# Linear attention plus a gated MLP on one core: loads on three queues, twelve tiles transposed by DMA, list order by landing times, the last tile in two pieces

## The chip, the core and the metric

The kernel runs on one core of a Trainium2 chip. The core has five engines with an instruction list each: TensorE (PE in the profile; its weight loads are shown apart as PEld), VectorE (DVE), ScalarE (ACT), GpSimd (POOL) and SyncE (SP), which here only issues DMAs. They meet through semaphores. Sixteen DMA engines move data between the chip's memory (HBM) and the core's on-chip memory, and within the latter. The metric is the device time of one execution, in microseconds (us).

## The reference

```
xn = (x - mean) / sqrt(var + 1e-5)                  # x: 2048 tokens x 512
# A: linear attention, 32 heads of 16
q, k, v = heads(xn @ wqkv)
pq, pk  = q @ w_phi[h], k @ w_phi[h]
phi(p)  = concat(softmax(p), softmax(-p))           # 32 features per head
kv, z   = sum_s phi(pk)^T v, sum_s phi(pk)
A       = (phi(pq) @ kv / (phi(pq) @ z + 1e-6)) @ wo
# B: gated MLP, F = 1792
B       = ((xn @ w_gate) * (xn @ w_up)) @ w_down
out     = x + A + B
```

All inputs and the output are bfloat16.

## The kernel before

Tokens are handled in 16 tiles of 128, one token per partition. A TensorE product needs the normalised tokens transposed (`xnT`: features on partitions). The stages:

- *Normalisation.* `emit_ln_stats` (L403) takes the statistics of a batch of tiles on VectorE (L406, L408), adds the epsilon on VectorE (L412) and raises to the power -1/2 on POOL (L414). The batches (L640) are tiles 0, 1, 2, 3 alone, then 4 to 7, 8 to 11, 12 to 15. `emit_xn` (L427) scales a tile on VectorE (L428) into a ring of four, transposes it on TensorE by four 128x128 products with the identity, and ScalarE copies the result from PSUM into `xnT`.
- *Weights folded.* `wprime` (L438) multiplies the transposed query and key weights (`wT`, loaded by a transposing DMA) with block-diagonal copies of `w_phi` (`wbd`, made on POOL, L384) into `Wp`, so that one product gives pq or pk.
- *Keys.* For each tile: V (`k_pe`), pk (`k_pk`), and `emit_exp` (L451): ScalarE copies p and -p, VectorE takes the maximum over features in a tree (L464), subtracts it (L470), ScalarE takes the exponential. `emit_sums` (L476) adds up in a tree on VectorE (L484); `k_norm` divides (L508, L511). `emit_kv` adds phi(pk)^T [v, 1] over eight tiles at a time.
- *MLP.* `glu` (L520) computes for a group g of four tiles and a block ft of 128 hidden units the gate and up products (eight matmuls of 512 columns); ScalarE copies the gate, VectorE multiplies (L533).
- *Queries.* `q_pk`, `emit_exp`, `q_scale`, a transposing DMA of the features (`q_T`), the products with kv (`q_num`), the division (L602, L603), a transposing DMA of the result (`q_oT`).
- *Output.* `final` (L616) accumulates 14 products with `w_down` and four with `wo`, 18 matmuls of 512 columns; VectorE adds x (L635) and SP stores the tile.

Each operation is recorded once with what it reads and writes (`_Sched`); nearly all matmuls thus carry the line L292, ScalarE's operations L273, DMA issues L162 (transposing) or L163. `_order` (L696) then plans: it goes through time with a price and a latency for each step, and on each engine takes the step that can start first, and among equals the one with the lowest priority number. Without an explicit priority that is the order of recording; `glu` has numbers from 1e6, `final` from 2e6, so that these two fill TensorE when nothing earlier is ready. A DMA is priced with 500 ns to issue, its bytes at 385 per ns behind what is queued, and 1400 ns:

```python
queued = dma_free > start + DMA_ISSUE + 200.0
dma_free = max(dma_free, start + DMA_ISSUE) + st.nbytes / DMA_RATE
st.finish = dma_free + DMA_LAT + (1000.0 if queued else 0.0)
```

The order that comes out is fixed in the program: at run time each engine goes through its list in that order and waits at each step for the semaphores that it needs.

All loads but the small `w_phi` are issued by SP, in this order: x tiles 0 to 1, 2 to 3, V weights, key weights (transposing), gate and up columns 0 to 511, x 4 to 7, query weights (transposing), x 8 to 15, the remaining gate and up columns, `w_down`, `wo`. TensorE starts with 50 products of a zeroed tile (L364), on which nothing depends.

Of the kernel before, what the change touches and what calls it, by code (L numbers as in the profile page):

```python
# [7 lines left out]
ACTF = mybir.ActivationFunctionType  # L8
# [58 lines left out]
class _Step:  # L67
    __slots__ = ("eng", "fn", "idx", "deps", "sig", "lane", "semval", "known", "waits", "is_out", "cost", "lat",
                 "seq", "finish", "prio", "nbytes")

    def __init__(self, eng, fn, idx, lane):
# [15 lines left out]
        self.nbytes = 0  # L87


class _Sched:  # L90
# [65 lines left out]
    def dma(self, eng, out_ap, in_ap, is_out=False, transpose=False, nbytes=131072, prio=None):  # L156
# [10 lines left out]
        st.nbytes = nbytes  # L167
# [26 lines left out]
def _build(nc, es, A_x, A_wqkv, A_w_phi, A_wo, B_w_gate, B_w_up, B_w_down, out):  # L194
# [73 lines left out]
    def act_op(out_ap, in_ap, func=ACTF.Copy, scale=1.0, bias=None, prio=None):  # L268
# [10 lines left out]
        return sc.step(ACT, fn, reads=r, writes=[out_ap], cost=50.0 + 0.833 * in_ap.free_size(), lat=180.0, prio=prio)  # L279
# [4 lines left out]
    def pool(fn, reads, writes, n, rate=2.0, prio=None):  # L284
        return sc.step(POOL, fn, reads=reads, writes=writes, cost=130.0 + rate * n, lat=120.0, prio=prio)
# [45 lines left out]
    def load_x(t0, n):  # L331
        sc.dma(SP, sbv("x", t0 * 512, n * 512).rearrange("p (t d) -> p t d", t=n),
               x_flat[t0 * 128:(t0 + n) * 128, :].rearrange("(t p) d -> p t d", p=128), nbytes=n * 131072)

    def load_w(dst, src, nbytes):
        sc.dma(SP, dst, src, nbytes=nbytes)

    def load_wT(w):

        sc.dma(SP, wT_v[:, w, :, :], A_wqkv[:, w * 512:(w + 1) * 512], transpose=True, nbytes=524288)  # L340

    def load_gu(f0, n):
        for v, src in ((wg_v, B_w_gate), (wu_v, B_w_up)):
            load_w(v[:, :, f0 * 128:(f0 + n) * 128],
                   src[:, f0 * 128:(f0 + n) * 128].rearrange("(q p) f -> p q f", p=128), n * 131072)

    sc.dma(ACT, wphi_v, bass.AP(tensor=A_w_phi.tensor, offset=A_w_phi.offset, ap=[[16, 128], [2048, NQ], [1, 16]]),
           nbytes=16384)
    load_x(0, 2)
    load_x(2, 2)  # L350
    load_w(wv_v, A_wqkv[:, 1024:1536].rearrange("(q p) j -> p q j", p=128), 524288)
    load_wT(1)
    load_gu(0, 4)
    load_x(4, 4)
    load_wT(0)
    load_x(8, 8)
    load_gu(4, 10)
    load_w(wd_v, B_w_down.rearrange("(f p) j -> p f j", p=128), NF * 131072)
    load_w(wo_v, A_wo.rearrange("(q p) j -> p q j", p=128), 524288)


    warm = sbv("tree", 0, 128)
    dve(lambda e: e.memset(warm, 0.0), [], [warm], 128)
    mms([(bank(7, 0, 128), warm, warm, True, True)] * 50, warm=True)  # L364
# [18 lines left out]
    for jt in range(NQ):  # L383
        pool(lambda e, jt=jt: e.tensor_tensor(  # L384
            out=wbd_v[:, jt, :].rearrange("p (g f b) -> p g f b", g=2, b=4),
            in0=wphi_v[:, jt, None, :, None].to_broadcast([128, 2, 16, 4]),
            in1=bind8.rearrange("p (g b) -> p g b", g=2)[:, :, None, :].to_broadcast([128, 2, 16, 4]), op=ALU.mult),
            [bind8, wphi_v[:, jt, :]], [wbd_v[:, jt, :]], 128)
# [3 lines left out]
        [maskh], [eps4], 4)  # L392

# [9 lines left out]
    def emit_ln_stats(t0, n):  # L403
# [3 lines left out]
        for t in range(t0, t0 + n):  # L407
# [4 lines left out]
        dve(lambda e: e.tensor_scalar(out=veps.unsqueeze(2), in0=var4, scalar1=1e-5, scalar2=None, op0=ALU.add),  # L412
            [mv_v[:, ts, :]], [veps], n)
        pool(lambda e: e.tensor_tensor(out=rstd4, in0=veps.unsqueeze(2), in1=mhalf[:, 0:n].unsqueeze(2), op=ALU.pow),  # L414
             [veps, mhalf], [rstd_v[:, ts, 0:1]], n, rate=150.0)
# [176 lines left out]
    def q_T(t):  # L592
        sc.dma(SP, eT(t), eq(t), transpose=True, nbytes=2 * 262144)
# [15 lines left out]
    def q_oT(t):  # L609
        o = sbv("oring", (t % 2) * 512, 512)  # L610
        sc.dma(SP, oT_v[:, :, t * 128:(t + 1) * 128], o, transpose=True, nbytes=2 * 131072)
# [36 lines left out]
    for t0, n in batches:  # L648
        emit_ln_stats(t0, n)
        for t in range(t0, t0 + n):  # L650
            emit_xn(t)
            k_pe(t)
# [183 lines left out]
```

## Time and profile before

| | us |
|---|---|
| three runs, median (lowest, highest) | 229.64 (229.61, 229.78) |
| the profiled execution | 230.12 |
| its span, from the first to the last instruction | 228.0 |
| TensorE busy | 219.0 |
| VectorE busy | 193.7 |
| ScalarE busy | 119.7 |
| POOL busy | 8.2 |

The profile is of one execution. The busy time of TensorE counts matmuls that overlap in its pipeline, so the pace is better read from the starts of weight loads. In a timeline a row merges neighbouring instructions of one kind on one engine: start, length, engine, line, operation, output and inputs, number; in brackets the idle time of the engine before it, and what ended that. The strip of DMA digits gives the busy share of the sixteen DMA engines in 40 slices of 5.7 us, in tenths. In the list of DMA issues the last number of a row is the median time from the issue's start to the landing.

### The profile page before, as it was taken

The page shows a single profiled execution, that of the slowest core. Times are in us where ns is not written, and L with a number is a line of the kernel's source. Part 1 is how long each engine was busy: PE and PEld are TensorE (multiplying, and loading weights), DVE is VectorE, ACT ScalarE, POOL GpSimd, SP SyncE. Part 2 cuts the span into 40 slices and gives each one's busy share as a digit, 9 for nine tenths or more (in the row PEclk, how much of TensorE's full clock was granted, in tenths as well). Part 3 has the DMA queues.
Part 4 walks back from the last instruction along what each step waited for, and adds up shares of the span by engine and source line. Part 5 has one row for each costly group of instructions (what it writes and reads, how often), then busy time and mean ns, then how long its engine had stood idle before and what let it go on. Part 6 is the DMA issues. An engine that isn't in the chain of part 4 may idle for free.

```text
span 228.0 us, 3617 instructions
## 1 busy us (share of the span) xinstructions
PE 219.0 (96%) x1306; PEld 108.9 (48%) x1330; DVE 193.7 (85%) x554; ACT 119.7 (52%) x201; POOL 8.2 (4%) x22
## 2 busy tenths in 40 slices
PE   8899799999999999999999999999999999998994
PEld 8454354444454555444464444444445444444441
DVE  4548999999997999999986999999999999993321
ACT  2587997735449987944528585464653331110000
POOL 5301000000011000000000000000000000000000
PEclk9999999999999999999999999999999999999999
DMA  6999970000000000000000035554144545468301
GB/s 181 249 285 369 379 249 1 0 0 0 0 3 1 0 3 0 0 3 0 0 4 0 0 65 96 85 94 103 36 92 105 118 92 116 92 126 110 88 23 46
DMA packets 39697, 18.33 MB, mean 80 GB/s; under 512 B 30720, under 2 KB 38656, under 8 KB 39680
## 3 DMA queue, kind: packets, MB, share of 16 engines
q1 hardware_dynamic: 39152, 18.09, 32.5%
q8 instruction: 10, 0.16, 0.3%
q10 hardware_dynamic: 528, 0.02, 0.1%
q14 instruction: 7, 0.06, 0.1%
HBM read 8.67 MB, written 2.10 MB: 47 GB/s over the span
## 4 chain that ended last, share of the span: by engine, by line
PE 85%; SPq 6%; DMA 5%; DVE 1%; issue 1%; ACT 1%
PE ps L292 85%; SPq L162 4%; DMA arena<-in_A_x_dram 3%; DMA arena<-arena 2%; SPq L163 1%; ACT arena L273 1%; DVE arena L464 1%; DVE arena L406 0%; DVE arena L635 0%; DVE arena L470 0%
## 5 line engine op out<-in xcount | busy, mean ns | idle before, releaser
L292 PE MATMUL ps<-arena 128*128 128x512 bf16 (+3 forms) x1306 | 219.0, 328 | 6.1 <-ACT arena L273 2.4
L292 PEld LDWEIGHTS ps<-arena 128*128 128x128 bf16 x1330 | 108.9, 100 | 115.7 <-DVE arena L533 2.3
L273 ACT ACTIVATE arena<-ps 128x512 bf16<-128x512 f32 (+1 forms) x168 | 88.0, 590 | 50.6 <-PE ps L292 45.7
L484 DVE TENSOR_TENSOR arena<-arena 128x512 f32<-128x512 bf16 (+3 forms) x128 | 49.3, 395 | 0.2
L273 ACT ACTIVATE arena<-arena 128x1024 bf16<-128x1024 bf16 x32 | 34.0, 1061 | 29.0 <-DVE arena L470 28.1
L533 DVE TENSOR_TENSOR arena<-ps,arena 128x512 bf16<-128x512 f32 x56 | 38.1, 681 | 2.2 <-PE ps L292 1.6
L464 DVE TENSOR_TENSOR arena<-arena 128x128 bf16<-128x128 bf16 (+3 forms) x128 | 31.7, 269 | 2.2 <-ACT arena L273 2.0
L470 DVE TENSOR_TENSOR arena<-arena 128x1024 bf16<-128x1024 bf16 x32 | 21.6, 676 | 0.0
L635 DVE TENSOR_TENSOR arena<-ps,arena 128x512 bf16<-128x512 f32 x16 | 11.0, 688 | 11.8 <-PE ps L292 11.5
L406 DVE BATCH_NORM_STATS2 arena<-arena 128x6 f32<-128x512 bf16 x16 | 10.5, 682 | 6.8 <-DMA arena<-in_A_x_dram 6.8
L603 DVE TENSOR_TENSOR arena<-ps,arena 128x512 bf16<-128x512 f32 x16 | 10.9, 680 | 0.1
L511 DVE TENSOR_TENSOR arena<-arena 128x1024 bf16<-128x1024 bf16 x16 | 10.9, 680 | 0.0
L602 DVE RECIPROCAL arena<-ps 128x32 f32<-128x32 f32 x16 | 5.6, 350 | 4.6 <-PE ps L292 4.3
L508 DVE RECIPROCAL arena<-arena 128x64 bf16<-128x64 f32 x16 | 8.7, 543 | 0.1
L428 DVE TENSOR_SCALAR arena<-arena 128x512 bf16<-128x512 bf16 x16 | 5.9, 409 | 2.2 <-POOL arena L414 2.0
L414 POOL TENSOR_TENSOR arena<-arena 128x1 f32<-128x1 f32 (+1 forms) x7 | 5.2, 750 | 60.7 <-DVE arena L412 60.7
L589 DVE TENSOR_TENSOR arena<-arena 128x512 bf16<-128x512 bf16 x16 | 6.6, 414 | 0.0
L586 DVE RECIPROCAL arena<-arena 128x32 f32<-128x32 f32 x16 | 5.5, 342 | 0.0
L587 DVE TENSOR_TENSOR arena<-arena 128x32 bf16<-128x32 f32 x16 | 2.7, 171 | 0.0
L273 ACT ACT_TABLE_LOAD x1 | 1.3, 1283 | 1.3 <-PEq L821 1.3
L408 DVE BATCH_NORM_AGGREGATE arena<-arena 128x2 f32<-128x6 f32 x16 | 1.9, 162 | 0.0
L551 DVE TENSOR_TENSOR arena<-arena 128x64 bf16<-128x64 f32 x8 | 1.7, 214 | 0.0
(18 smaller groups left out, 8.4 us busy)
## 6 DMA issues: line engine op xcount, KB each, us to landing
out_dram<-arena SPq DMA_DIRECT2D x16, 128.0 KB, 1.7
arena<-in_B_w_down_dram SPq DMA_DIRECT2D x1, 1792.0 KB, 15.4
arena<-in_B_w_gate_dram SPq DMA_DIRECT2D x1, 1280.0 KB, 9.1
arena<-in_B_w_up_dram SPq DMA_DIRECT2D x1, 1280.0 KB, 11.9
arena<-in_A_x_dram SPq DMA_DIRECT2D x1, 1024.0 KB, 6.5
arena<-in_A_x_dram SPq DMA_DIRECT2D x2, 256.0 KB, 3.2
arena<-in_A_wqkv_dram SPq DMA_DIRECT2D x1, 512.0 KB, 5.2
arena<-in_B_w_gate_dram SPq DMA_DIRECT2D x1, 512.0 KB, 4.4
```

Source lines behind the costliest of these rows:

```text
L162: return e.dma_start_transpose(out_ap, in_ap)
L273: return e.activation(out=out_ap, in_=in_ap, func=func, scale=scale, **kw)
L292: ins = e.matmul(o, lhsT=l, rhs=r, start=a, stop=z)
L406: dve(lambda e, t=t: e.bn_stats(stats_v[:, t, 0:6], x_tile(t)), [x_tile(t)], [stats_v[:, t, 0:6]], 512)
L464: dve(lambda e, dst=dst, src=src, k=k: e.tensor_tensor(out=dst, in0=src[:, :, 0:k], in1=src[:, :, k:2 * k], op=ALU.max), [src], [dst], 16 ...
L470: dve(lambda e: e.tensor_tensor(out=p4, in0=p4, in1=src[:, :, None, :].to_broadcast([128, 16, 16, 4]), op=ALU.subtract), [pst, src], [pst] ...
L484: dve(lambda e, dst=dst, src=src, k=k: e.tensor_tensor(out=dst, in0=src[:, :, 0:k], in1=src[:, :, k:2 * k], op=ALU.add), [src[:, :, 0:2 * ...
L508: dve(lambda e: e.reciprocal(out=rs, in_=sm), [sm], [rs], 64, rate=8.0)
L511: dve(lambda e: e.tensor_tensor(out=e4, in0=e4, in1=r4[:, :, None, :].to_broadcast([128, 16, 16, 4]), op=ALU.mult), [ek_v[:, t, :], rs], [ ...
L533: dve(lambda e: e.tensor_tensor(out=dst, in0=bank(bu), in1=gr, op=ALU.mult), [bank(bu), gr], [dst], 512, prio=-1.0)
L603: dve(lambda e: e.tensor_tensor(out=o.rearrange("p (g h d) -> p g h d", g=8, h=4), in0=nd[:, :, 0:64].rearrange("p g (h d) -> p g h d", h= ...
L635: dve(lambda e: e.tensor_tensor(out=og, in0=bank(b), in1=x_tile(t), op=ALU.add), [bank(b), x_tile(t)], [og], 512, prio=-2.0)
```

## The change

- The loads are spread over three queues. SP: x tile 0, tile 1, tiles 2 to 3, key weights, query weights (both transposing). ScalarE: `w_phi`, V weights, x 4 to 7, gate and up columns 0 to 511. POOL: x 8 to 15, the remaining gate and up columns, `w_down`, `wo`; these five are made to wait for the landing of x 4 to 7 and for the last `wbd` product.
- ScalarE gets a first Exp of a zeroed element; the warm-up has 46 products instead of 50.
- The four `wbd` products on POOL move behind the power of tile 3, each behind POOL's step before it.
- The epsilon is added on POOL instead of VectorE.
- Tiles 4 to 15 are transposed by a DMA on SP; tiles 0 to 3 stay on TensorE.
- The planner no longer models the bytes: each load carries a time `at` at which it is taken to have landed, each issue a price, each transposing DMA a latency. Prices of some ScalarE, POOL and reciprocal steps are changed.
- In `final` the three matmul pieces have one priority, and tile 15 is computed and stored in two pieces, columns 0 to 383 and 384 to 511, in two PSUM banks.

The diff, cut to its core:

```diff
-    def dma(self, eng, out_ap, in_ap, is_out=False, transpose=False, nbytes=131072, prio=None):
+    def dma(self, eng, out_ap, in_ap, is_out=False, transpose=False, issue=500.0, land=1700.0, at=0.0, prio=None):
...
+        st.cost = issue
+        st.lat = land
+        st.at = at
...
-        return sc.step(ACT, fn, reads=r, writes=[out_ap], cost=50.0 + 0.833 * in_ap.free_size(), lat=180.0, prio=prio)
+        return sc.step(ACT, fn, reads=r, writes=[out_ap], cost=(50.0 if str(in_ap.tensor.name) == "ps" else 95.0) + 0.833 * in_ap.free_size(),
+                       lat=180.0, prio=prio)
...
-    def pool(fn, reads, writes, n, rate=2.0, prio=None):
-        return sc.step(POOL, fn, reads=reads, writes=writes, cost=130.0 + rate * n, lat=120.0, prio=prio)
+    def pool(fn, reads, writes, n, rate=1.8, fixed=130.0, prio=None):
+        return sc.step(POOL, fn, reads=reads, writes=writes, cost=fixed + rate * n, lat=120.0, prio=prio)
...
+    def load_w(on, dst, src, at):
+        return sc.dma(on, dst, src, at=at, issue=500.0 if on != POOL else 850.0)
+
+    def load_wT(w, at):
+
+        sc.dma(SP, wT_v[:, w, :, :], A_wqkv[:, w * 512:(w + 1) * 512], transpose=True, at=at, issue=4600.0)
...
+    load_x(SP, 0, 1, 2900.0)
+    load_x(SP, 1, 1, 3500.0)
+    load_x(SP, 2, 2, 4500.0)
+    load_wT(1, 9500.0)
+    load_wT(0, 15000.0)
     sc.dma(ACT, wphi_v, bass.AP(tensor=A_w_phi.tensor, offset=A_w_phi.offset, ap=[[16, 128], [2048, NQ], [1, 16]]),
-           nbytes=16384)
-    load_x(0, 2)
-    load_x(2, 2)
-    load_w(wv_v, A_wqkv[:, 1024:1536].rearrange("(q p) j -> p q j", p=128), 524288)
-    load_wT(1)
-    load_gu(0, 4)
-    load_x(4, 4)
-    load_wT(0)
-    load_x(8, 8)
-    load_gu(4, 10)
-    load_w(wd_v, B_w_down.rearrange("(f p) j -> p f j", p=128), NF * 131072)
-    load_w(wo_v, A_wo.rearrange("(q p) j -> p q j", p=128), 524288)
-
-
-    warm = sbv("tree", 0, 128)
-    dve(lambda e: e.memset(warm, 0.0), [], [warm], 128)
-    mms([(bank(7, 0, 128), warm, warm, True, True)] * 50, warm=True)
+           at=4200.0)
+    one = sbv("lnt", 4 * NT, 1)
+    zero = sbv("tree", 0, 128)
+    dve(lambda e: e.memset(zero, 0.0), [], [zero], 128)
+    act_op(one, zero[:, 0:1], func=ACTF.Exp)
+    load_w(ACT, wv_v, A_wqkv[:, 1024:1536].rearrange("(q p) j -> p q j", p=128), 6500.0)
+    x4_loaded = load_x(ACT, 4, 4, 9000.0)
+    load_gu(ACT, 0, 4, 12500.0)
+
+
+    mms([(bank(7, 0, 128), zero, zero, True, True)] * 46, warm=True)
...
+    def make_wbd():
+        for jt in range(NQ):
+            pool(lambda e, jt=jt: e.tensor_tensor(
...
+                [bind8, wphi_v[:, jt, :]], [wbd_v[:, jt, :]], 128).deps.append(sc.by_eng[POOL][-2])
+
+    def load_rest():
+        wbd_made = sc.by_eng[POOL][-1]
+        late = [load_x(POOL, 8, 8, 15500.0)]
+        late += load_gu(POOL, 4, 10, 23000.0)
+        late.append(load_w(POOL, wd_v, B_w_down.rearrange("(f p) j -> p f j", p=128), 30000.0))
+        late.append(load_w(POOL, wo_v, A_wo.rearrange("(q p) j -> p q j", p=128), 32000.0))
+        for st in late:
+            st.deps += [x4_loaded, wbd_made]
...
-        dve(lambda e: e.tensor_scalar(out=veps.unsqueeze(2), in0=var4, scalar1=1e-5, scalar2=None, op0=ALU.add),
-            [mv_v[:, ts, :]], [veps], n)
+        pool(lambda e: e.tensor_scalar(out=veps.unsqueeze(2), in0=var4, scalar1=1e-5, scalar2=None, op0=ALU.add),
+             [mv_v[:, ts, :]], [veps], n)
...
+        if t >= 4:
+            sc.dma(SP, xnT_v[:, :, t * 128:(t + 1) * 128], xn_tile(t), transpose=True, issue=1250.0, land=3200.0)
+            return
         b = next_a()
...
-        dve(lambda e: e.reciprocal(out=rs, in_=sm), [sm], [rs], 64, rate=8.0)
+        dve(lambda e: e.reciprocal(out=rs, in_=sm), [sm], [rs], 64, rate=6.0)
...
-        sc.dma(SP, eT(t), eq(t), transpose=True, nbytes=2 * 262144)
+        sc.dma(SP, eT(t), eq(t), transpose=True, issue=1250.0, land=3300.0)
...
-        sc.dma(SP, oT_v[:, :, t * 128:(t + 1) * 128], o, transpose=True, nbytes=2 * 131072)
+        sc.dma(SP, oT_v[:, :, t * 128:(t + 1) * 128], o, transpose=True, issue=1250.0, land=3200.0)
...
+        c0, c1 = cols
+        ob = bank(b, c0, c1 - c0)
+        items = [(hT(g, ft, lo, 128), wd_v[:, ft, c0:c1]) for ft in range(NF)]
+        items += [(oT_v[:, q, t * 128:(t + 1) * 128], wo_v[:, q, c0:c1]) for q in range(NQ)]
+        items = group(ob, items)
+        for k in (0, 7, 14):
+            mms(items[k:k + 7], prio=base)
...
+        if t0 == 3:
+            make_wbd()
+            load_rest()
...
-    for t in range(NT):
+    for t in range(NT - 1):
         final(t, 7 if t < 4 else (7, 5, 6)[t % 3])
+    final(NT - 1, 7, (0, 384))
+    final(NT - 1, 5, (384, 512))
...
-            free_at[e] = start + DMA_ISSUE
-            queued = dma_free > start + DMA_ISSUE + 200.0
-            dma_free = max(dma_free, start + DMA_ISSUE) + st.nbytes / DMA_RATE
-            st.finish = dma_free + DMA_LAT + (1000.0 if queued else 0.0)
+            free_at[e] = start + st.cost
+            st.finish = max(start + st.lat, st.at)
```

## The prediction

> **What bounds the kernel now.** I read the page first, then the chain of work that ended last, then the timeline of TensorE's weight loads (PEld; every matmul has one, and none is missing), and last the timelines of SP and VectorE in the first 26 us.
>
> From the page: the span, TensorE's share, the idle time before matmuls, the DMA queues and two landings.
>
> ```profile
> span 228.0 us, 3617 instructions
> PE 219.0 (96%) x1306; PEld 108.9 (48%) x1330; DVE 193.7 (85%) x554; ACT 119.7 (52%) x201; POOL 8.2 (4%) x22
> DMA  6999970000000000000000035554144545468301
> ...
> PE 85%; SPq 6%; DMA 5%; DVE 1%; issue 1%; ACT 1%
> ...
> arena<-in_A_x_dram SPq DMA_DIRECT2D x1, 512.0 KB, 6.2
> arena<-arena SPq DMA_TRANSPOSE x32, 3.1
> arena<-in_A_wqkv_dram SPq DMA_TRANSPOSE x2, 7.8
> ```
>
> TensorE works 96% of the span and carries 85% of the chain: only what takes work or idle time off TensorE, or shortens what stands before its first and after its last matmul, can pay. VectorE (85%) is the next bound. The sixteen DMA engines are full from slice 2 to slice 6 (up to 34 us) and nearly idle until 131 us.
>
> TensorE's weight loads at the start and at the end, from the timeline:
>
> ```profile
> 6.73 0.23 PEld L292 LDWEIGHTS ps<-arena 128*128 128x128 bf16 x4 [0.44 <-DVE arena L428]
> 7.26 0.23 PEld L292 LDWEIGHTS ps<-arena 128*128 128x128 bf16 x4 [0.30 <-DVE arena L428]
> ...
> 18.85 3.90 PEld L292 LDWEIGHTS ps<-arena 128*128 128x128 bf16 x28 [0.70 <-DVE arena L428]
> 24.86 1.22 PEld L292 LDWEIGHTS ps<-arena 128*128 128x128 bf16 x10 [2.10 <-DVE arena L533]
> ...
> 208.01 2.31 PEld L292 LDWEIGHTS ps<-arena 128*128 128x128 bf16 x19 [1.30 <-DMA arena<-arena]
> ...
> 218.03 6.57 PEld L292 LDWEIGHTS ps<-arena 128*128 128x128 bf16 x31
> ```
>
> The last row gives the rate: 30 steps in 6.47 us, 0.216 us for a 512-column matmul. The first two give the price of a transpose on TensorE: four in 0.23 us. Between 25 and 225 us TensorE stands still for one wait worth the name (the 1.30 before 208.01); at the start there are two (0.70, 2.10), and in both the releaser is VectorE.
>
> Why VectorE is late there, from the timelines of SP and VectorE:
>
> ```profile
> 2.32 4.54 SPq L162 DMA_TRANSPOSE arena<-in_A_wqkv_dram  x1
> ...
> 8.07 0.51 SPq L163 DMA_DIRECT2D arena<-in_A_x_dram  x1
> 8.62 5.39 SPq L162 DMA_TRANSPOSE arena<-in_A_wqkv_dram  x1
> ...
> 17.82 7.99 SPq L163 DMA_DIRECT2D arena<-in_A_wo_dram  x1
> ```
>
> ```profile
> 14.30 2.47 DVE L406 BATCH_NORM_STATS2 arena<-arena 128x6 f32<-128x512 bf16 x4 [4.78 <-DMA arena<-in_A_x_dram]
> ...
> 18.39 1.38 DVE L428 TENSOR_SCALAR arena<-arena 128x512 bf16<-128x512 bf16 x4 [0.53 <-POOL arena L414]
> 19.69 0.42 DVE L464 TENSOR_TENSOR arena<-arena 128x512 bf16<-128x512 bf16 x1
> ```
>
> One queue issues all loads. The load of tokens 4 to 7 goes out at 8.07 us, behind a weight transpose that holds the queue for 4.54 us, and lands at 14.3. VectorE has idled 4.78 us by then, does the statistics of these tiles, and only at 19.69 starts the softmax work of the first tile. From there it is busy to about 209 us.
>
> **The change part by part.** Gains are against the profiled execution, whose time is 230.12 us for a span of 228.0; the median of the three runs, 229.64, is 0.48 lower, and I take the same gain off it.
>
> *Start.* Four warm-up matmuls fewer are 4 x 0.107 = 0.43 us (the 50 of before take 5.41). TensorE also idles 0.27 between the warm-up and the first transposes. Tile 0, loaded alone, should land between 2.5 us (0.8 plus 1.7, the page's landing of a 128 KB store) and the 3.9 of the two-tile load; I take 3.3. Then statistics 0.69 and 0.16, POOL 0.2 for the added epsilon (small POOL rows are 0.10 to 0.19) and 0.55 for the power, scaling 0.47, hand-overs 0.2: 5.6, before the warm-up ends at 6.0. Gain 0.7, bounds -0.4 and 0.7: the warm-up steps by 0.107 where the transposes after it step by 0.057, and if the faster pace came no earlier than before, at 6.7, real work would run at half pace until then. Of the smaller waits up to 11 us (0.30, 0.33, 0.48) I count 0.4 as gained, since tiles 2 and 3 come while earlier products run.
>
> *Transposes.* Tiles 4 to 15 lose four transposes each: 12 x 0.23 = 2.7 us of TensorE, and ScalarE 12 evictions of 0.6, which are hidden (ScalarE is busy 52%). In their place SP issues 12 DMA transposes. The 32 of before land after 3.1 us, idle DMA engines about them; tiles 8 to 15 find this too (slices 8 to 23 are empty), and the matmuls of loaded tiles cover them. Tiles 4 to 7 fall into the full slices: 3.1 at best, 7.8 at worst by the weight transposes. These move four times the bytes, so I take 4.
>
> *Tokens 4 to 7, three queues.* On ScalarE's queue wv goes out after the table load (1.30 plus 1.28), x 4 to 7 next, then the first gate and up columns; these issues (0.5 each) and the early Exp (0.24) lie in ScalarE's idle 4.59 us before 7.17. By order alone x 4 to 7 take the place of the first gate load, which landed at 6.91 + 4.4 = 11.3; right behind wv (1.82 + 5.2 = 7.0) they would land at 8.5, as 512 KB follow each other by 1.45 (gate 11.3, up 12.8, x 14.3). I take 9.5, as the issue no longer waits for the weight transpose.
> The Trainium skill's page "DMA: Bandwidth & Descriptors", section "Issuing engines are not separate DMA queues", says that several issuing engines save only the time the sequencer takes to issue, as all loads run on the same DMA engines. By it I would take the 11.3, and the sum below would be some 1.8 smaller.
>
> POOL now waits for x 4 to 7 and for its own wbd products (1.47, moved behind the fourth power), then issues five loads; behind these, in its order as the planner's prices put it, stand the epsilon and power of tiles 4 to 7, for which xn 4 to 7, SP's transposes and the products of tile 4 wait. No POOL issue is in this trace. Bounds from SP's rows: 0.5 each, and 7.99 where the queue is full. I take the planner's own 0.85, near the many short rows: 9.5 + 4.25 = 13.8, power 1.2 with epsilon, scaling 0.5, transpose 4: tile 4 lies transposed at 19.5. The statistics (2.8) hide beside the issues. TensorE's other work up to there: 6.0 + tiles 0 to 3 transposed 0.9, their V and score products 6.9, W' for keys 0.9, four gate-up pairs 6.9, W' for queries 0.9, bubbles 1 = 23.5. So there is cover, but the lists run in order, and the planner (landing 3.2) puts tile 4's product near 18: 0.9 of new waits, bounds 0 and 13.
> The Trainium skill's page "SBUF — State Buffer", section "Who interferes with whom", has VectorE in its two-port modes shut GpSimd out, descriptor writing included. If the four scalings (0.41 each) and no more did this, it would be 1.6 later; no run here shows it yet.
>
> With x 4 to 7 done early the waits of 0.70 (for xn 4) and 1.64 (TensorE's own idle time under the 2.10) go: 2.3. Late next is VectorE's softmax chain, which should start near 14.5, after the first score product, some 5 us earlier, less 1.2 for the scalings that now follow.
>
> *Order elsewhere.* The planner's new prices cost nothing themselves, they only move list entries. Seven epsilon additions (1.1) leave VectorE. I take nothing for this, nor for the 1.30 before 208 (a transpose of 4.9 instead of 3.1); bounds -2 and +1.3.
>
> *Last tile.* Eighteen matmuls of 512 become 18 of 384 and 18 of 128: 3.9 both ways, weight loads at 0.057 keeping pace. The last addition falls from 0.69 to about 0.28 (between 0.21 for 65 columns and 0.41 for 256); the first piece's addition and store run beside the second piece. The last store stays at 1.7. Gain 0.4.
>
> Sum: 0.7 + 0.4 + 2.7 + 2.3 - 0.9 + 0.4 = 5.6: 224.5 against 230.12, 224.0 against the median.
>
> **Rivals.**
> *VectorE holds the end.* In the profile 14.2 us of TensorE work follow the last numerator product (210.9 to 225.1), which waits for VectorE's chain. If that chain starts only 3 us earlier (x 4 to 7 at 11.3), TensorE's savings turn into waits for it: 3 + 0.4 gives 226.2. For it: VectorE is busy 176 of the 189 us between 25 and 214. Against: finals can be put ahead of the last numerators, and TensorE has work to spare there.
> *Tiles 4 to 7 late, the other sign.* POOL's issues block as SP's did at 17.82. With three issues of 0.85, one of 7.99 and one more, POOL is free at 20.9, tile 4 transposed at 25 or later, and TensorE, in order, waits from about 18.5: 6.5 us. The 2.3 are not gained then, 3.3 of gains remain: 229.64 + 3.2 = 232.8. It is slower from a wait of 3.3 us on, tile 4 transposed after 22. For it: 5.9 MB queued at once. Against: most issue rows are half a microsecond.
> *A smaller wait of this kind*, 2 us more than I took: 226.0.
> *The loads gain nothing*: the DMA engines are full either way, tokens 4 to 7 still land past 13, and the transposes' 2.7 return as waits on landings: 229.4.
>
> **How the numbers follow.** Forecast 0.58, with a range of its own of 222.3 to 225.5; VectorE 0.16; the smaller wait 0.12; the late tiles 0.11; no gain 0.03. All gains at once, with the 1.30 and no new wait, are 5.6 + 0.9 + 1.3: 221.8, so I start the range a little under that, at 221.3, and end it at 228.3, which leaves out the slower case, the no-gain case and little else. A difference of under 0.2% (0.46 us; the three runs span 0.17) can't be told from none. Faster 0.86, same 0.03, slower 0.11.
>
> **What would show it.** Statistics of tile 4 before 10 us, not 14.30; POOL's five issues done by 14; no transposes on TensorE past tile 3; weight loads of tile 4's V product without an idle row over 1 us; no 2.10 near 24.86; first softmax row of VectorE near 14.5; last addition under 0.3. Wrong, if a wait on a DMA landing over 3 us stands on TensorE between 16 and 30 us, or if TensorE idles before numerator products from 195 us on.

## The result and the profile after

| | before | changed |
|---|---|---|
| median of the runs, us (lowest, highest) | 229.71 (229.61, 229.94) | 243.31 (242.55, 243.77) |
| the profiled execution, us | 230.12 | 242.55 |
| its span, us | 228.0 | 241.1 |

The changed kernel takes 1.059 times as long (95% interval 1.057 to 1.061): 13.6 us slower, where 5.6 us less had been forecast. One execution of a later kernel (246.12 us, under "Both, and the last tile's pieces in order") fell in a slower state of the chip and is left out of that kernel's median. The first reading is the page of the changed kernel.

```profile
span 241.1 us, 3562 instructions
...
PE 220.8 (92%) x1273; PEld 106.4 (44%) x1296; DVE 192.0 (80%) x548; ACT 114.4 (47%) x190; POOL 14.4 (6%) x34
...
PEclk9799756999999999999999999999999999999999
DMA  6999990000000440000000035465336356762101
...
PE 57%; DVE 23%; DMA 12%; issue 3%; ACT 3%; SPq 0%; DVEq 0%
```

VectorE and ScalarE are busy a little less than before. What is new is in the strip of the granted TensorE clock: a dip in slice 2 (6 to 12 us) and one in slices 5 to 7 (24 to 42 us). From the page of the kernel before, the same strip, all nines, and the row of its two-tile loads of x for comparison further down:

```profile
PEclk9999999999999999999999999999999999999999
...
arena<-in_A_x_dram SPq DMA_DIRECT2D x2, 256.0 KB, 3.2
```

And the chain that ended last, 85% TensorE before, now runs through DMA landings (12%) and VectorE (23%). The list of waits (engine and line, what it waited for, total in us, times, longest) names the events:

```profile
PEld ps L296 <- DMA arena<-arena: 13.5, 5, 9.7
...
DVE arena L501 <- ACT arena L276: 12.8, 3, 11.7
...
PEld ps L296 <- DVE arena L442: 3.2, 1, 3.2
```

The 9.7 is a wait for a DMA from on-chip memory to on-chip memory: a transpose of a token tile. VectorE's 11.7 is its echo, since VectorE then has no scores to work on. The 3.2 is at the start, for the scaling of tile 0. First the start, from the timeline:

```profile
7.37 1.29 DVE L420 BATCH_NORM_STATS2 arena<-arena 128x6 f32<-128x512 bf16 x2 [2.59 <-DMA arena<-in_A_x_dram]
8.57 0.72 DVE L442 TENSOR_SCALAR arena<-arena 128x512 bf16<-128x512 bf16 x2
9.02 0.59 PEld L296 LDWEIGHTS ps<-arena 128*128 128x128 bf16 x8 [3.15 <-DVE arena L442]
...
10.94 0.15 PEld L296 LDWEIGHTS ps<-arena 128*128 128x128 bf16 x1 [0.28 <-issue]
...
13.48 1.12 POOL L164 DMA_DIRECT2D arena<-in_A_x_dram  x1 [0.63 <-POOL arena L393]
...
14.11 0.24 PEld L296 LDWEIGHTS ps<-arena 128*128 128x128 bf16 x4 [0.48 <-DMA arena<-in_A_wqkv_dram]
...
17.18 0.76 POOL L164 DMA_DIRECT2D arena<-in_A_wo_dram  x1
...
20.18 11.75 SPq L163 DMA_TRANSPOSE arena<-arena  x4
21.03 0.42 DVE L481 TENSOR_TENSOR arena<-arena 128x512 bf16<-128x512 bf16 x1
```

VectorE's list has the statistics of tiles 2 and 3 ahead of the scaling of tile 0 (L442). The planner had been told that these tiles land at 4.5 us; they land at 7.3. TensorE idles 3.15 us after its warm-up, starts its transposes at 9.02 (6.73 before), and then runs at half pace: from 10.51 to 12.64 us its weight loads start 0.43 us apart instead of 0.216, and the granted clock is 0.50 there. The list of DMA issues shows what else is late:

```profile
arena<-in_A_x_dram SPq DMA_DIRECT2D x1, 256.0 KB, 5.6
...
arena<-in_A_wqkv_dram SPq DMA_TRANSPOSE x2, 9.2
```

Two tiles of x took 5.6 us (3.2 before), the transposed weights 9.2 (7.8 before); the key weights landed at 13.8 us (TensorE's row at 14.11 waits for them), where they had landed at 8.9. They lost that time to ScalarE's loads, packet by packet: between 8.5 and 11.5 us the DMA records of SP's queue hold 786 packets of 256 bytes of the key weights, those of ScalarE's queue 750 of 1024 bytes. From 13 to 14.5 us, with no other queue at work, 1682 packets of 256 bytes go by, over four times the rate. Then tile 4, on the weight loads:

```profile
33.18 0.13 PEld L296 LDWEIGHTS ps<-arena 128*128 128x128 bf16 x2 [9.66 <-DMA arena<-arena]
...
35.98 0.13 PEld L296 LDWEIGHTS ps<-arena 128*128 128x128 bf16 x2 [1.81 <-DMA arena<-arena]
36.38 0.15 PEld L296 LDWEIGHTS ps<-arena 128*128 128x128 bf16 x1 [0.28 <-issue]
```

The four transposes were issued from 20.18 on (the SPq row above) and landed at 33.1, 35.9, 36.4 and 36.8: 13 us for the first, against 2.4 to 4.3 for tiles 8 to 15 later in the same execution. The 0.28 in the last row, repeated for each load up to 40 us, is the half pace: a step of 0.43 instead of 0.216. The granted clock stood at half from 26.5, while TensorE still waited, to 40.2. Windows of the two kernels (length, busy time with instruction counts of PE, PEld, DVE, ACT, POOL, granted clock, DMA share, GB/s), the changed one first:

```profile
25.00:47.00 22.00, 12.85 (x57) 5.68 (x59) 9.12 (x26) 9.14 (x16) 0.00 (x0) 0.69 0.57 148
47.00:79.00 32.00, 31.59 (x145) 13.19 (x147) 32.00 (x83) 17.30 (x27) 1.28 (x2) 1.00 0.02 4
```

```profile
25.00:47.00 22.00, 21.84 (x115) 10.57 (x117) 21.95 (x57) 18.62 (x32) 0.00 (x0) 1.00 0.37 122
47.00:79.00 32.00, 31.84 (x165) 15.17 (x166) 30.32 (x83) 19.91 (x34) 2.02 (x2) 1.00 0.00 1
```

From 25 to 47 us TensorE gets through 59 weight loads instead of 117. From 47 to 79 VectorE is busy without a gap, 32.00 of 32, and TensorE gets through 147 where there were 166: the score work that VectorE could not do during the wait now holds TensorE up. In the starts of weight loads the delay against before is 2.3 us at the first transposes, 3.6 at the scores of tile 3 (17.41 to 21.05), 14.5 at the first hidden units of group 1 (51.69 to 66.18), and 12.9 at the end; the transposes that left TensorE give a little back on the way.

At the end nothing is gained either:

```profile
237.81 0.76 DVE L647 TENSOR_TENSOR arena<-ps,arena 128x384 bf16<-128x384 f32 x2 [3.02 <-PE ps L296]
```

The two pieces of the last tile were interleaved on TensorE, so both additions come at the very end, one behind the other. From TensorE's last result to the end of the span it is 3.1 us, against 2.9 before.

### The profile page after: what moved, and what is told of

Same layout as the page of the kernel before. It is cut to its first block, busy times and chain, and to the rows that moved or that the text cites. A ratio compares the mean times of both kernels' runs of the same rounds, so it can differ in the third digit from the quotient of the medians.

```text
span 241.1 us, 3562 instructions
## 1 busy us (share of the span) xinstructions
PE 220.8 (92%) x1273; PEld 106.4 (44%) x1296; DVE 192.0 (80%) x548; ACT 114.4 (47%) x190; POOL 14.4 (6%) x34
## 4 chain that ended last, share of the span: by engine, by line
PE 57%; DVE 23%; DMA 12%; issue 3%; ACT 3%; SPq 0%; DVEq 0%
PE ps L296 57%; DMA arena<-arena 9%; DVE arena L550 7%; DVE arena L501 5%; DVE arena L481 3%; ACT arena L276 3%; DMA arena<-in_A_x_dram 2%; DVE arena L487 2%; DVE arena L525 1%; DVE arena L528 1%; DVE arena L442 1%; DVE arena L420 1%; DVE arena L620 1%; DVE arena L606 0%; DVE arena L603 0%
## 5 line engine op out<-in xcount | busy, mean ns | idle before, releaser
L296 PE MATMUL ps<-arena 128*128 128x512 bf16 (+4 forms) x1273 | 220.8, 334 | 17.2 <-DMA arena<-arena 10.8
L296 PEld LDWEIGHTS ps<-arena 128*128 128x128 bf16 x1296 | 106.4, 100 | 131.4 <-DMA arena<-arena 13.5
L276 ACT ACTIVATE arena<-ps 128x512 bf16<-128x512 f32 (+1 forms) x156 | 82.4, 584 | 63.2 <-PE ps L296 55.6
L501 DVE TENSOR_TENSOR arena<-arena 128x512 f32<-128x512 bf16 (+3 forms) x128 | 50.3, 397 | 12.9 <-ACT arena L276 12.8
L276 ACT ACTIVATE arena<-arena 128x1024 bf16<-128x1024 bf16 (+1 forms) x33 | 34.1, 1035 | 30.2 <-DVE arena L487 28.5
L550 DVE TENSOR_TENSOR arena<-ps,arena 128x512 bf16<-128x512 f32 x56 | 38.2, 683 | 5.5 <-ACT arena L276 4.9
L647 DVE TENSOR_TENSOR arena<-ps,arena 128x512 bf16<-128x512 f32 (+2 forms) x17 | 11.0, 654 | 15.8 <-PE ps L296 15.8
L528 DVE TENSOR_TENSOR arena<-arena 128x1024 bf16<-128x1024 bf16 x16 | 10.9, 682 | 0.0
L620 DVE TENSOR_TENSOR arena<-ps,arena 128x512 bf16<-128x512 f32 x16 | 10.8, 675 | 0.1
L442 DVE TENSOR_SCALAR arena<-arena 128x512 bf16<-128x512 bf16 x16 | 6.2, 413 | 1.1 <-POOL arena L428 1.0
L426 POOL TENSOR_SCALAR arena<-arena 128x1 f32<-128x1 f32 (+1 forms) x7 | 1.5, 225 | 67.9 <-DVE arena L422 67.9
(23 smaller groups left out, 13.8 us busy)
```

What stands on the lines that cost most here:

```text
L276: return e.activation(out=out_ap, in_=in_ap, func=func, scale=scale, **kw)
L296: ins = e.matmul(o, lhsT=l, rhs=r, start=a, stop=z)
L442: dve(lambda e: e.tensor_scalar(out=xn_tile(t), in0=x_tile(t), scalar1=mv_v[:, t, 0:1], scalar2=rstd_v[:, t, 0:1], op0=ALU.subtract, op1=A ...
L501: dve(lambda e, dst=dst, src=src, k=k: e.tensor_tensor(out=dst, in0=src[:, :, 0:k], in1=src[:, :, k:2 * k], op=ALU.add), [src[:, :, 0:2 * ...
L528: dve(lambda e: e.tensor_tensor(out=e4, in0=e4, in1=r4[:, :, None, :].to_broadcast([128, 16, 16, 4]), op=ALU.mult), [ek_v[:, t, :], rs], [ ...
L550: dve(lambda e: e.tensor_tensor(out=dst, in0=bank(bu), in1=gr, op=ALU.mult), [bank(bu), gr], [dst], 512, prio=-1.0)
```

## The experiments

**Tiles 4 to 7 transposed on TensorE again.**

```diff
-        if t >= 4:
+        if t >= 8:
             sc.dma(SP, xnT_v[:, :, t * 128:(t + 1) * 128], xn_tile(t), transpose=True, issue=1250.0, land=3200.0)
```

> The changed kernel, but tiles 4 to 7 are transposed on TensorE again; 8 to 15 stay with the DMA. Theory 1 (the DMA transposes of tiles 4 to 7 share the DMA engines packet for packet with POOL's loads, whose packets are 4 to 5 KB, and so land 13 us after their issue; TensorE waits for them and then runs at half pace): the waits of 9.6 and 1.9 us and about 1.9 us of half pace after them go, four tiles cost 0.9 on TensorE, so 243.3 - 13.4 + 0.9 = 230.8. Rival (the new list order or the late start is the main loss): it stays above 237.

Measured 233.91 (before on the same chip 229.70; ratio 1.019, interval 1.014 to 1.023). Of 13.6 us, 9.4 go with the DMA transposes of four tiles. It stays 3 above the expectation, and its waits are those of the start and then of landings: 2.4 us for the key weights, which landed at 15.9 in this run, and 1.7 at 72.7 us for a DMA transpose.

**The later loads held until tile 7 is transposed.**

```diff
+    def load_last():
+        turned = sc.by_eng[SP][-1]
+        late = load_gu(POOL, 4, 10, 34000.0)
+        late.append(load_w(POOL, wd_v, B_w_down.rearrange("(f p) j -> p f j", p=128), 41000.0))
+        late.append(load_w(POOL, wo_v, A_wo.rearrange("(q p) j -> p q j", p=128), 43000.0))
+        for st in late:
+            st.deps.append(turned)
...
             emit_xn(t)
+            if t == 7:
+                load_last()
```

> The changed kernel, but the remaining gate and up columns, w_down and wo are issued only when the DMA transpose of tile 7 has landed; the planner is told landings of 34, 41 and 43 us for them. Theory 1: with no load in flight the four transposes land about 3 us after their issues (issued near 20.2, landed near 23.3 and up to 1.3 apart), TensorE's wait of 9.6 us goes, and the time is 230 to 232, unless the gate and up columns now come late (needed near 34). Rival (SBUF transposes of this size are slow whenever four follow each other, or SP's queue holds them): they still land 8 us or more after their issue and the time stays above 238.

Measured 232.97 (1.015, 1.009 to 1.021). SP's row and TensorE's weight loads:

```profile
16.11 5.67 SPq L163 DMA_TRANSPOSE arena<-arena  x4
```

```profile
19.01 10.92 PEld L296 LDWEIGHTS ps<-arena 128*128 128x128 bf16 x63
```

The transposes stay where they were; only the traffic beside them is gone, apart from the end of x 8 to 15. The first lands at 21.9, 5.8 us after its issue, where 3 had been expected, the other three 0.5 apart (5.0, 4.2 and 3.4 after theirs), and TensorE takes 63 weight loads across that stretch without a row of idle time. So it is the loads in flight, not the transposing DMA or four in a row. The time stays 1 us above the expected range. One new wait shows:

```profile
40.24 0.55 PEld L296 LDWEIGHTS ps<-arena 128*128 128x128 bf16 x4 [2.76 <-ACT arena L276]
```

The gate and up columns that were held back had landed by then, at 30.1 and 33.5. ScalarE's copy stood 2.81 us behind VectorE's sums, and the chain runs through VectorE from 28 to 39 us.

**The size of the other queue's packets.** The remaining gate and up columns, `w_down` and `wo` go out on ScalarE's queue.

```diff
-        late += load_gu(POOL, 4, 10, 23000.0)
+        late += load_gu(ACT, 4, 10, 23000.0)
...
-        late.append(load_w(POOL, wd_v, B_w_down.rearrange("(f p) j -> p f j", p=128), 30000.0))
-        late.append(load_w(POOL, wo_v, A_wo.rearrange("(q p) j -> p q j", p=128), 32000.0))
+        late.append(load_w(ACT, wd_v, B_w_down.rearrange("(f p) j -> p f j", p=128), 30000.0))
+        late.append(load_w(ACT, wo_v, A_wo.rearrange("(q p) j -> p q j", p=128), 32000.0))
```

> The changed kernel, but the remaining gate and up columns, w_down and wo are issued on ScalarE's queue instead of POOL's (x 8 to 15 stays on POOL). Theory 1a (the DMA engines alternate packet for packet, so what counts is the size of the other queue's packets): ScalarE's packets are 1 to 2.5 KB (46 to 105 ns) instead of 4 to 5 KB (190 to 210 ns); a tile's 32 packets for each DMA engine then need 32 x (20 + 46 to 105 ns) = 2.1 to 4.0 us instead of 7, and the four transposes land within 9 to 16 us of the first issue's start of data, the first of them within 6 us of its issue. Rival 1b (transposes yield to any other load, whatever its packets): the first lands 10 us or more after its issue, again only when the loads end. ScalarE may be held by its own issues, so the total says little: 236 to 245.

One execution: 241.25, and the transposes, issued from 16.39 on, landed at 26.6, 28.8, 32.3 and 34.3. By landing times alone the rival 1b is nearer: the first came 10.2 us after its issue. The packets decide it. The DMA records of the traces, counted in stretches where a transposing queue and one other are at work (records of 4 bytes left out):

```
kernel, stretch              transposing queue      other queue
changed, 27.5 to 29.5 us     158 packets of 256 B   159 of 4096 B (POOL),    mean 189 ns
this one, 23 to 26 us        386 packets of 256 B   418 of 2560 B (ScalarE), mean 103 ns
this one, 27 to 29 us        504 packets of 256 B   532 of 1024 B (ScalarE), mean  49 ns
before, 132 to 134.5 us     1024 packets of 256 B   none
```

One packet of the one queue, one of the other, in all three sizes. A tile is 512 packets, 32 for each DMA engine. At 79 a microsecond, beside POOL's packets, it would take 6.5 us; at 129 beside 2560 bytes, 4.0; at 252 beside 1024 bytes, 2.0; alone, at 410, 1.2. So the rate was as expected, and what I had left out is a delay before the first packet: 4.0 us after SP's issue in the changed kernel and 4.3 here, 2.2 with the loads held, 1.2 with idle DMA engines. Where it comes from isn't settled. For the first tile of the changed kernel the sum closes: 4.0 to the first packet, 7.7 until 512 packets are through, 1.3 to the landing, 13.0 in all. The total says nothing here, since ScalarE itself was held for 8.4 us by its last issue:

```profile
PEld ps L296 <- ACT arena L276: 12.3, 12, 8.2
...
ACT arena L276 <- issue: 7.9, 1, 7.9
```

**Only the planner is told 13 us for those transposes.**

```diff
-xn_tile(t), transpose=True, issue=1250.0, land=3200.0)
+xn_tile(t), transpose=True, issue=1250.0,
+                   land=13000.0 if t < 8 else 3200.0)
```

> The changed kernel, but the planner is told that the DMA transposes of tiles 4 to 7 take 13 us instead of 3.2. Only list order changes. Theory 1 with cover: TensorE's list has the gate-up pairs 2 and 3 and the query weights ahead of tile 4 (some 4.3 us of work), so the wait of 9.6 falls to about 5 and the time to about 238. Rival (the work ahead of tile 4 is held up by the same loads or by VectorE): no gain, 242 to 244.

Measured 235.93 (1.026, 1.024 to 1.029): 7.4 us less than the changed kernel, by list order alone. The transposes land as late as ever (36.1 to 37.4), but TensorE has other work in front and no longer waits for them. These 7.4 and the 9.4 of the first experiment are for the most part one wait, avoided in two ways, and don't add up. What is left sits elsewhere: waits of 2.6 us for the key weights up to 15.9, 3.7 for a DMA transpose up to 94.5, 1.9 for another up to 160.2.

**Only the planner is told 7.4 us for x tiles 2 and 3.**

```diff
-    load_x(SP, 2, 2, 4500.0)
+    load_x(SP, 2, 2, 7400.0)
```

> The changed kernel, but the planner is told that x tiles 2 and 3 land at 7.4 us instead of 4.5; nothing but list order changes. Theory 2 (VectorE's list has the statistics of tiles 2 and 3, which land at 7.3, ahead of the scaling of tile 0; TensorE idles 2.9 us and then runs at half pace to 12.9): TensorE's first transposes begin at 6.0 to 6.4 instead of 9.0 and its products there run at full pace. The wait for tile 4 takes most of this back, as it ends with the loads: total gain 0 to 2, 241.3 to 243.3. Rival (the start is bound by the landing of the V weights at 7.4 anyway): first V product not before 9.5, no change.

Measured 241.24 (1.054, 1.049 to 1.059), 2.1 us less than the changed kernel.

```profile
6.26 0.23 PEld L296 LDWEIGHTS ps<-arena 128*128 128x128 bf16 x4 [0.89 <-DVE arena L442]
...
10.99 0.23 PEld L296 LDWEIGHTS ps<-arena 128*128 128x128 bf16 x4 [2.23 <-DVE arena L442]
```

The late start was VectorE's list order, as theory 2 has it: the transposes begin at 6.26. But tiles 2 and 3 still land at 7.9, so a wait of 2.23 comes at 10.99 with half pace behind it. "Full pace" in the expectation held only up to there. Most of the gain then goes to the next told landing that isn't met, as VectorE's rows show:

```profile
21.30 1.29 DVE L420 BATCH_NORM_STATS2 arena<-arena 128x6 f32<-128x512 bf16 x2 [8.22 <-DMA arena<-in_A_x_dram]
...
23.69 1.37 DVE L442 TENSOR_SCALAR arena<-arena 128x512 bf16<-128x512 bf16 x4
```

x 8 to 15 are told 15.5 and land at 21.3, the new list has their statistics ahead of the scaling of tiles 4 to 7, and VectorE stands 8.22 us. The scaling comes at 23.69 (19.74 in the changed kernel), and the wait for tile 4 grows to 11.7.

**Both, and the last tile's pieces in order.**

```diff
-            mms(items[k:k + 7], prio=base)
+            mms(items[k:k + 7], prio=base + (c0 > 0))
```

with the edits of the first and the previous experiment.

> The changed kernel with tiles 4 to 7 transposed on TensorE, the planner told 7.4 us for x tiles 2 and 3, and the second piece of the last tile after the first in priority. If theories 1 and 2 hold and add up: 230.8, less 2.9 of idle time and 1.2 of half pace at the start, less 0.4 at the end: 226.3. If the start is bound elsewhere: 230.4.

Measured 237.58 (1.034, 1.030 to 1.038): a miss, slower than the first experiment alone. TensorE starts at 6.25, but then waits 2.1 us at 10.9, 2.8 at 23.2 for the scaling of tile 4, and 2.5 and 2.1 between 90 and 98 us for tiles 12 to 15, whose transposes SP got at 90.9 to 94.7.

```profile
20.31 1.29 DVE L420 BATCH_NORM_STATS2 arena<-arena 128x6 f32<-128x512 bf16 x2 [7.31 <-DMA arena<-in_A_x_dram]
```

It is the wait of the previous experiment again: VectorE stands 7.31 us for x 8 to 15, told 15.5 and landed at 20.3, with the scaling of tiles 4 to 7 behind. In the first experiment VectorE's list had the scaling first. So correcting one told landing moved the loss to the next wrong one. Why tiles 12 to 15 come late was not taken further; I went on to the loads.

**One part alone: tiles 8 to 15 by DMA, in the kernel before.**

```diff
+        if t >= 8:
+            sc.dma(SP, xnT_v[:, :, t * 128:(t + 1) * 128], xn_tile(t), transpose=True, nbytes=2 * 131072)
+            return
         b = next_a()
```

> The kernel before with one part of the change: tiles 8 to 15 are transposed by DMA (DMA engines idle around them), all else as before. Theory: the transposes themselves are sound, 8 x 0.23 = 1.9 us leave TensorE: 227.8. Rival (landings of 2.4 to 4.4 us turn into waits on TensorE in the list order): 229 to 231.

Measured 227.89, before 229.81 (0.992, 0.989 to 0.994): 1.9 us less, the price of eight tiles by the sum. Where the DMA engines are idle the transposes are worth what the prediction took for them.

**One part alone: the last tile in two pieces, the second after the first, in the kernel before.**

```diff
-    for t in range(NT):
+    for t in range(NT - 1):
         final(t, 7 if t < 4 else (7, 5, 6)[t % 3])
+    final(NT - 1, 7, (0, 384))
+    final(NT - 1, 5, (384, 512))
```

> The kernel before with one part of the change: the last tile in two pieces, the second after the first in priority. In the changed kernel the pieces were interleaved on TensorE and the stretch from the last matmul's end to the end of the span was 3.1 us, 2.9 before. Theory (the order of the pieces took the gain): with the pieces one after the other the last addition is 0.28 instead of 0.69 and nothing stands before its store; gain 0.4: 229.3. Rival (a store of 256-byte rows is slower to land and takes the gain): 229.7 or more.

Measured 228.89, before 229.60 (0.9968, 0.9955 to 0.9982).

```profile
224.22 0.56 DVE L637 TENSOR_TENSOR arena<-ps,arena 128x384 bf16<-128x384 f32 x1 [2.23 <-PE ps L292]
224.81 1.07 SPq L163 DMA_DIRECT2D out_dram<-arena  x2
225.23 0.29 DVE L637 TENSOR_TENSOR arena<-ps,arena 128x128 bf16<-128x128 f32 x1 [0.45 <-PE ps L292]
```

The first piece's addition is over before the second's begins, the last one is 0.29, and the span ends 2.3 us after TensorE's last result instead of 2.9: 0.6 in the trace, 0.7 in the runs. In the changed kernel, with its 3.1, the interleaving had taken this gain.

**All loads back on one queue.** On top of the first experiment and of the pieces in order:

```diff
+    load_x(SP, 0, 1, 3100.0)
+    load_x(SP, 1, 1, 3700.0)
+    load_x(SP, 2, 2, 4700.0)
...
+    load_w(SP, wv_v, A_wqkv[:, 1024:1536].rearrange("(q p) j -> p q j", p=128), 7100.0)
+    load_wT(1, 9000.0)
+    load_x(SP, 4, 4, 10500.0)
+    load_gu(SP, 0, 4, 14300.0)
+    load_wT(0, 17600.0)
+    load_x(SP, 8, 8, 20600.0)
+    load_gu(SP, 4, 10, 27200.0)
+    load_w(SP, wd_v, B_w_down.rearrange("(f p) j -> p f j", p=128), 32400.0)
+    load_w(SP, wo_v, A_wo.rearrange("(q p) j -> p q j", p=128), 33800.0)
```

> The changed kernel with all loads back on one queue in the order of before, only x 4 to 7 ahead of the first gate and up columns, planned landings set to what one queue gave; tiles 4 to 7 transposed on TensorE; second piece of the last tile after the first. Theory 3 (the spread itself delays what is needed first, since the DMA engines were already full: x 2 to 3 from 4.7 to 7.3 us, key weights from 8.9 to 13.8): both land as before again, TensorE's transposes start near 6.2, and with tiles 8 to 15 off TensorE and the earlier x 4 to 7 the time is 224.5 to 227.5. Rival (the planner's new prices make bad lists whatever the loads do): above 229.

Measured 226.79, before 229.81 (0.986, 0.985 to 0.988): 3.0 us faster than before and 7.1 faster than the first experiment, of which the pieces in order are 0.7. The key weights land at 9.0 again, x 2 to 3 at 5.6, x 4 to 7 at 11.3. So about 6.4 us went with the three queues and with the told landings that belonged to them; this run doesn't part the two. The planner's new prices, which stay, are not the harm. The start is still behind a told landing that is too early (4.7 for 5.6), hence the next.

> The kernel with all loads on one queue (226.8), but the planner is told 5.7 us for x tiles 2 and 3, as they landed there, instead of 4.7. Only list order changes. In that kernel TensorE idled from 6.0 to 7.3 for the scaling of tile 0, behind the statistics of tile 2, and ran at half pace from 7.5 to 10.9. Expected: first transposes at 6.2, no half pace, 1.1 of idle time and about 1 of half pace less: 224.7 to 225.5. Rival (the first V product waits for its weights at 7.1, ScalarE and VectorE are late next): 226 to 227.

With 5.7 told for x tiles 2 and 3, and nothing else changed: 225.04, before 229.60 (0.981, 0.979 to 0.983). In this profile the two tiles landed at 4.7, not 5.6, so how much of the 1.75 us is list order alone stays open. The page, and the start of the weight loads:

```profile
PE 218.2 (98%) x1312; PEld 107.9 (48%) x1312; DVE 192.2 (86%) x548; ACT 116.1 (52%) x194; POOL 10.1 (5%) x29
...
PEclk9999999999999999999999999999999999999999
```

```profile
6.08 0.35 PEld L296 LDWEIGHTS ps<-arena 128*128 128x128 bf16 x4 [0.22 <-DVE arena L446]
...
15.00 10.93 PEld L296 LDWEIGHTS ps<-arena 128*128 128x128 bf16 x61 [1.38 <-ACT arena L276]
```

TensorE is busy 98% of the span, at full clock throughout; the only wait over 1 us left is the 1.38 at 15 us, ended by a copy of ScalarE's, just after the up columns, which x 4 to 7 now precede, had landed at 14.8. This is the fastest kernel of the study, 4.6 us under the one before.

**Which queue does the harm.** The one-queue kernel (with 4.7 told), but x 8 to 15 and everything after the query weights back on POOL, told 15.5 and so on as in the change.

```diff
-    load_x(SP, 8, 8, 20600.0)
-    load_gu(SP, 4, 10, 27200.0)
-    load_w(SP, wd_v, B_w_down.rearrange("(f p) j -> p f j", p=128), 32400.0)
-    load_w(SP, wo_v, A_wo.rearrange("(q p) j -> p q j", p=128), 33800.0)
+            load_rest()
```

> The kernel with all loads on one queue (226.8), but x 8 to 15, the remaining gate and up columns, w_down and wo back on POOL, waiting for x 4 to 7 as in the change; SP keeps the rest. It asks which of the two added queues does the harm once the DMA transposes of tiles 4 to 7 are gone. If it is ScalarE's (it lets x 4 to 7 and gate and up columns overtake x 2 to 3 and the key weights): x 2 to 3 land near 5.6, key weights near 9, and the time is 226 to 228.5. If POOL's large packets harm as well: the query weights, which a DMA transposes while POOL's loads run, land after 20 instead of 16.1, and the time is 229 or more.

Measured 231.65 (1.008, 1.006 to 1.011), 4.9 more than with one queue. It doesn't answer the question:

```profile
13.35 0.36 DVE L422 BATCH_NORM_AGGREGATE arena<-arena 128x2 f32<-128x6 f32 x4
20.87 0.69 DVE L420 BATCH_NORM_STATS2 arena<-arena 128x6 f32<-128x512 bf16 x1 [7.16 <-DMA arena<-in_A_x_dram]
21.48 1.36 DVE L442 TENSOR_SCALAR arena<-arena 128x512 bf16<-128x512 bf16 x4
```

x 8 to 15 landed at 20.9, as with one queue (20.8), but the planner had been told 15.5, and VectorE stood 7.16 us before its statistics with the scaling of tiles 4 to 7 behind it. The query weights did land later, at 20.1 instead of 16.1 and 18.1 in the two one-queue kernels; their packets were through at 15.3, and only the 4-byte records that close the transfer came between 17.9 and 19.6. What shows clearly is that with ScalarE's queue gone x 2 to 3 land at 4.9 and the key weights at 8.7: it was that queue which delayed them. POOL's can't have: in the changed kernel its first load went out at 13.48.

**The change as it is, with the landings of its own profile told.**

```diff
-    load_x(SP, 2, 2, 4500.0)
-    load_wT(1, 9500.0)
-    load_wT(0, 15000.0)
+    load_x(SP, 2, 2, 7400.0)
+    load_wT(1, 13800.0)
+    load_wT(0, 15600.0)
...
-    load_gu(ACT, 0, 4, 12500.0)
+    load_gu(ACT, 0, 4, 13100.0)
...
-        late = [load_x(POOL, 8, 8, 15500.0)]
+        late = [load_x(POOL, 8, 8, 20600.0)]
```

and so on for the others, 13 us for the transposes of tiles 4 to 7, and the last tile's pieces in order.

> The changed kernel with its queues and transposes as they are, but the planner is told the landings that the profile of the changed kernel shows: x 3.1, 3.9, 7.4, V weights 7.4, x 4 to 7 9.3, gate and up 13.1, key and query weights 13.8 and 15.6, x 8 to 15 20.6, the rest 28.1, 33.9, 35.5, transposes of tiles 4 to 7 13 us; the second piece of the last tile comes after the first. If the wrong landings in the lists are all of the harm, it falls to 229.7 or below. If the spread and the transposes under load cost by themselves, the two largest waits (9.6 for tile 4, 2.9 for tile 0) go but key weights, tiles 4 to 7 and VectorE's chain still come later than before: 231 to 235.

Measured 234.06 (1.018, 1.016 to 1.020), inside the second range. So the lists carry 9.3 us of the 13.6 together with the last tile's 0.7; the rest, 4.4 us against before and 9 against the fastest one-queue kernel, is left to transport and to landings that were missed again, which this run doesn't part: in its own run the key weights landed at 16.1 (told 13.8), the first up columns at 16.1 (13.1), x 2 to 3 at 8.1 (7.4). Over the eight kernels with three queues the key weights landed between 13.7 and 16.1 us, over the six that load them from SP's queue without ScalarE's loads beside it between 8.2 and 9.2.

## Why the prediction was wrong, point by point

*What bounds the kernel, and what the parts are worth* was right where a part could be tried alone: eight tiles off TensorE gave 1.9 us (8 x 0.23 = 1.84 in the sum); the pieces in order gave 0.7, where 0.4 was taken.

*The step that failed is "Tiles 4 to 7 fall into the full slices: 3.1 at best, 7.8 at worst by the weight transposes. These move four times the bytes, so I take 4."* The first took 13.0. The row I took as the upper bound came from a kernel with a single queue, where a transpose waits its turn and then has the DMA engines to itself. With a second queue at work the engines alternated packet by packet in these traces, so the rate of a transpose, in packets of 256 bytes, is set by the other queue's packets, and those of POOL's loads are of 4096 and 5120 bytes. With 4.0 us before the first packet, 7.7 for the 512 and 1.3 after them that made the 13.0. The trace of before had no two busy queues but ScalarE's 16 KB, so the bound should have been left open upwards. My own sign of being wrong came true: a wait on a DMA landing over 3 us, on TensorE, from 23.5 to 33.2 us. Taking these four transposes away gave 9.4 us, holding the loads beside them 10.3.

*The second failed step is one that is missing.* I priced what the three queues do for tokens 4 to 7 (9.5 taken, 9.24 measured) and gave no price to what they do to everything else on engines that the DMA strip showed full. x 2 to 3 went from 4.7 to 7.3 us and the key weights from 8.9 to 13.8. The gain of 0.7 at the start thus became a loss of 2.3 at the first transposes. Tile 0 itself was as predicted, landed at 3.1 for 3.3; its scaling waited in VectorE's list behind tiles 2 and 3. I had read from the diff that the lists follow told landings and not asked what happens when one isn't met; with its own landings told, the change is 9.3 us better, 0.7 of it the last tile. The V weights' issue was misread too: it did not wait for the table load but went out at 1.34, beside it.

*The page that I weighed against the row.* The Trainium skill's "DMA: Bandwidth & Descriptors", section "Issuing engines are not separate DMA queues", held in total: the last load landed at 35.5 us (33.8 before), and x 4 to 7 came at 9.24, sooner than the 11.3 that I would have taken by it, only as others came later. The Trainium skill's same page, section "Queues, rings and completion order", has each engine go round the queues at packet granularity. The traces agree, with 158 packets against 159, 386 against 418 and 504 against 532. That sentence was the rule to weigh against this change, and I didn't. As to the Trainium skill's "SBUF — State Buffer", section "Who interferes with whom", no run here shows whether VectorE holds up POOL's issues; they took 0.75 to 1.12.

*POOL.* Its five issues took 4.5 us (4.25 taken), so the case of issues that block did not come. They began at 13.5, though, not 9.5: the `wbd` products stood behind the power of tile 3, and that behind the late x 2 to 3.

*New waits of 0.9, bounds 0 and 13.* They were 9.7 and 1.8, and the granted clock fell to half 3 us into the first. The bound held for the single wait; the half pace I had bounded only at the start, by 0.4, and by the steps of 0.43 instead of 0.216 it cost about 1.2 there and 1.9 after tile 4. The VectorE chain was to start at 14.5 and started at 21.0.

*The rivals.* "Tiles 4 to 7 late, the other sign" had the place, the sign and the consequence in list order, with 0.11 and 232.8, but another cause. "VectorE holds the end" came in another form, from 47 to 79 us, as a consequence of the wait.

## What to carry to other kernels

Here the DMA engines were already full, and more queues moved nothing faster in total: they decided who waits, and a transpose in small packets beside loads in large ones waited most. Put such a transpose where the trace shows the engines idle, and keep the loads that are needed first alone on one queue. An instruction order that is fixed from expected landings is only as good as these: one landing told 3 us too early cost the wait and half pace behind it, correcting it alone moved the loss to the next wrong one, and told landings must be read again from the profile of the kernel that they produce.

## What the runs showed of the hardware that was not expected

- In three stretches with a second queue the DMA queues alternated packet for packet, at 1024, 2560 and 4096 bytes. At the paces measured there, the 512 packets of a tile's transpose need 1.2 us alone, 2.0 beside 1 KB packets, 4.0 beside 2.5 KB, 6.5 beside 4 KB.
- Under load the first packet of a new transpose started 4.0 to 4.3 us after its issue, against 1.2 with idle engines; the cause stays open.
- The same load landed at different times from kernel to kernel: the key weights 2.4 us apart over the eight kernels with three queues and 1.0 over the six without ScalarE's loads, the query weights 5.2 apart over the eight and 1.9 over the five with one queue.
- TensorE's granted clock was at half for 3.4 us or longer around waits of 2.1 to 11.7 us. But it stayed full around the wait of 2.10 at 24.86 in the kernel before, and its weight loads kept stepping by 0.216 after a wait of 3.9 at 21.9 (x 8 to 15 and the rest on POOL) and of 3.3 at 36.6 (own landings told). What decides isn't shown here.
